# Weight conversion in a fused attention and expert kernel: the shift moved from GpSimd to VectorE, the subtractions from VectorE to GpSimd, and two thirds of the conversions held behind attention blocks

## The chip, the cores and the metric

The kernel runs on one core of a Trainium2 chip. The metric is device time in microseconds (us) of one execution; the number for the kernel before is the median of three runs. The engines are called by the names of the profile: PE is TensorE (PEld its weight loads), DVE is VectorE, ACT is ScalarE, POOL is GpSimd, SP is SyncE.

## What is computed

The reference first runs causal attention with a memory term, then a gated feed-forward layer on its result. Sizes: 4 batches, 8 heads, 576 positions, head size 64; then 2304 rows of 512, hidden width 1536.

```python
scores = scale * q @ k.T;  scores = where(causal, -1e9, scores) - max
local  = softmax(scores) @ v
mem    = (phi(q) @ M_prev) / (phi(q) . z_prev + 1e-6)      # phi(x) = elu(x) + 1
x      = g * mem + (1 - g) * local                        # g = sigmoid(beta), per head
xn     = x / rms(x) * rms_g
out    = (silu(xn @ w_gate) * (xn @ w_val)) @ w_out
```

The three weight matrices arrive as 64-bit floats and are read by the kernel as pairs of 32-bit words.

## The kernel before, in words

**Rows and blocks.** The 2304 rows are 18 blocks of 128. A block goes through: scores on PE (line 449), masking and row minimum on DVE (line 455), exponent on ACT (line 501), a split of the probabilities P into a high and a low f16 part (ACT line 503, then a subtraction in `u_lo`, line 512, on DVE or POOL), a transpose of P, and the product with v (lines 536 to 538). `mem_mm` adds the memory part and `loc_evac` sums the two halves of the heads on POOL (line 611). `x_norm` squares the block on ACT (line 220) and makes the scale on POOL (lines 621 and 624); `x_split` casts the block to two f16 parts, with `hi_cast` on ACT (line 82) and `lo_cast` on DVE (line 85), and transposes it into `xT`. Blocks 0 and 1 are transposed by PE, with an eviction copy (`evict`, lines 348 to 353) that goes to ACT and DVE in turn; all later blocks are transposed by a DMA on SP's queue.

**Feed-forward.** Two blocks form a chunk of 256 rows, so there are 9 chunks. For each of 12 slices of the hidden width `m_proj` makes gate and value (line 765, 24 matmuls), `m_act` and `m_split` the activation in two f16 parts (lines 771 to 775, 796, 797), and `m_down` adds to the output (lines 819 to 821). The first projection needs `xT` of blocks 0 and 1 and the split first third of the gate and value weights.

**Weights.** Gate and value weights come in 24 pieces of 128 x 512, numbered so that pieces 0 to 7, 8 to 15 and 16 to 23 are the three thirds of the hidden width; w_out comes in 12 pieces. A piece is loaded into a ring of 5 slots (`RING`; the load of piece p+5 is issued once piece p has been converted, the first five loads on SP's queue, the rest on ACT's). `f64_to_f32` converts it in three steps: ACT turns the upper words into the float's upper bits (line 690), POOL turns the lower words into 3 bits by a multiplication and a minimum, in place (line 692), DVE shifts and joins both (line 695). Four matmuls on PE (line 135) then sum squares of the piece, which give a scale for the third (`gv_scales`, from line 705). After that `split` (lines 89 to 104) makes two f16 parts. Way "0" is a scaled cast on ACT (line 82) and a subtraction with scale on DVE (line 85). Way "3" is a scaling in place on DVE (line 99), a plain cast on ACT (line 101) and a subtraction on POOL (line 104). `SPLIT` gives the way: in each third of gate and value the pieces alternate between "0" and "3"; all of w_out takes "0". The f16 parts of piece p are written where the f32 data of piece p-1 lay, so the cast of a piece comes after the last read of the piece before it.

**Order.** The attention steps are a list with weights, `A`; the weight and feed-forward steps are emitted in four stretches (`run`, lines 1053 to 1062) and the attention steps between them up to a goal. Attention steps of blocks 0 and 1, then of 2 and 3, get a higher priority (`PRIO`). The tile framework's scheduler fixes the order of each engine's queue from these priorities and its own timing model, so the order of emission is not the order on the engine. `paced` adds an order of its own: a load of piece p after the conversion of piece p-5.

Of the kernel before, what the change touches and what calls it, by code (L numbers as in the profile page):

```python
# [13 lines left out]
U32 = mybir.dt.uint32  # L14
I64 = mybir.dt.int64
AF = mybir.ActivationFunctionType
ALU = mybir.AluOpType
# [14 lines left out]
A3 = 0.2  # L32
A4 = 0.3
C2 = 8
SPLIT = ("03", "03", "03", "0")
VWAY = "11"
RING = 5
PACE = 5
NTP = 2
PRIO = (500, 600, 100)  # L40
NPM = 2
NPOOL = (4, 8)
# [3 lines left out]
def attn_memory_moe_kernel(  # L46
# [12 lines left out]
    nc = tc.nc  # L59
# [7 lines left out]
    NC = DM // P  # L67
# [11 lines left out]


    def hi_cast(dst, src, scale):
        nc.scalar.activation(dst, src, AF.Copy, scale=scale)

    def lo_cast(dst, src, scale, hi):
        nc.vector.scalar_tensor_tensor(
            out=dst, in0=src, scalar=scale, in1=hi, op0=ALU.mult, op1=ALU.subtract
        )

    def split(dst_hi, dst_lo, src, scale, way="0"):


        if way == "0":
            hi_cast(dst_hi, src, scale)
            lo_cast(dst_lo, src, scale, dst_hi)
            return
        if way in "12":
            nc.scalar.activation(src, src, AF.Copy, scale=scale)
        else:
            nc.vector.tensor_scalar(src, src, scale, None, op0=ALU.mult)
        if way in "135":  # L100
            nc.scalar.copy(dst_hi, src)
        else:
            nc.vector.tensor_copy(dst_hi, src)
        nc.gpsimd.tensor_tensor(dst_lo, src, dst_hi, ALU.subtract)
# [69 lines left out]
    blocks = []  # L174
# [150 lines left out]
    def prep_M(b):  # L325
        src = qst.pop(("M", b)).rearrange("p (h e) -> p h e", h=H)
        held.pop(("M", b), None)
        m = sb.tile([P, 2, H, D + 2], F16, tag="M16", name=f"M16_{b}")
        M16[b] = m
        c = consts_of(b) if b < 2 else cb[b]  # L330
        hi_cast(m[:, 0, :, :D], src, c[:, 2:3])
        lo_cast(m[:, 1, :, :D], src, c[:, 2:3], m[:, 0, :, :D])
        nc.gpsimd.tensor_copy(m[:, :, :, D], zhl[:, :, b * H : (b + 1) * H])
# [9 lines left out]
        split(t[:, :, 0, :], t[:, :, 1, :], s3, scale, way)  # L343
        return t

    turn = [0]

    def evict(dst, src):
        turn[0] += 1
        if turn[0] % 2:  # L350
            nc.scalar.copy(dst, src)
        else:
            nc.vector.tensor_copy(dst, src)

    def tposed(dst, src, n):

        if n >= NTP:
            nc.sync.dma_start_transpose(out=dst, in_=src)
            return
        for j0 in range(0, src.shape[1] // P, 4):  # L360
            t = ps.tile([P, 4, P], F32, tag="gv", name="tp")
            for j in range(4):
                w = src[:, (j0 + j) * P : (j0 + j + 1) * P]
                nc.tensor.matmul(t[:, j, :], w, id16, start=True, stop=True)
            evict(dst[:, j0 : j0 + 4, :], t)
# [19 lines left out]
    def prep_q(n):  # L385
        t = split_rows(qst[n], qsc[n][:, 0:1])
        qT[n] = sb.tile([P, 2, H, P], F16, tag="qT", name=f"qT{n}")
        tposed(qT[n][:, 0], flat(t), n)
        if n < NTP:
            for j0 in range(0, H, 4):  # L390
                t = ps.tile([P, 4, P], F32, tag="gv", name="tp")
                nc.tensor.matmul(t, swap16, qT[n][:, 0, j0 : j0 + 4, :], start=True, stop=True)
                evict(qT[n][:, 1, j0 : j0 + 4, :], t)
            return
        nc.sync.dma_start(out=qT[n][D:, 1], in_=qT[n][:D, 0])
        nc.sync.dma_start(out=qT[n][:D, 1], in_=qT[n][D:, 0])
# [107 lines left out]
        Ssb[(n, h0)] = (s, G * w, p16)  # L504

    def lo_on_pool(n, h0):
        return NPOOL[0] <= n < NPOOL[1] and h0 % NPM == 0

    def u_lo(n, h0):
        s, w, p16 = Ssb.pop((n, h0))  # L510
        eng = nc.gpsimd if lo_on_pool(n, h0) else nc.vector
        eng.tensor_tensor(p16[:, w : 2 * w], s[:, :w], p16[:, :w], ALU.subtract)  # L512
        pt = sb.tile([P, 2 * (NI + 1), P], F16, tag="PT", name="PT", bufs=LAG + 1)
        tposed(pt[:, : 2 * w // P, :], p16[:, : 2 * w], n)
        Pt[(n, h0)] = pt
# [111 lines left out]
    def x_split(n):  # L627
        x, ss = t1s.pop(n)
        x16 = sb.tile([P, 2, HD], F16, tag="row16", name="x16")
        hi_cast(x16[:, 0], x, ss)  # L630
        lo_cast(x16[:, 1], x, ss, x16[:, 0])
        c = n // 2
        if n % 2 == 0:
            xT[c] = sb.tile([P, 2 * NC, 2 * P], F16, tag="xT", name=f"xT{c}")
        tposed(xT[c][:, :, (n % 2) * P : (n % 2) * P + P], x16.rearrange("p t d -> p (t d)"), n)
# [6 lines left out]
    raws = {}  # L642
    NR = RING

    begun = {}

    def paced(ins, p):

        if p - PACE in begun:
            tc.add_manual_dep(  # L650
                ins.ins, begun[p - PACE].ins.name,
                mybir.DependencyInfo(mybir.DependencyClass.Sync, mybir.DependencyReason.SCHED_ONLY),
                reason="pace",
            )

    def hold(p, at):

# [4 lines left out]
    def load_w(m, cc, t):  # L662
        w = (w_gate, w_val)[m]
        p = piece(m, cc, t)
        raws[p] = hold(p, 2 * (p % NR))
        ins = (nc.sync if p < PACE else nc.scalar).dma_start(
            out=raws[p].bitcast(I64), in_=w[cc * P : (cc + 1) * P, t * 512 : (t + 1) * 512]
        )
        paced(ins, p)
# [12 lines left out]
    def f64_to_f32(raw, dst, p):  # L682

        r = raw.rearrange("p (f w) -> p f w", w=2)
        ri, di = r.bitcast(I32), dst.bitcast(I32)
        begun[p] = nc.scalar.activation(dst, r[:, :, 1], AF.Prelu, scale=2.0 ** -112, alpha=2.0 ** 32)  # L690

        nc.gpsimd.tensor_scalar(  # L692
            ri[:, :, 0], r.bitcast(U32)[:, :, 0], 2.0 ** -29, 7.0, op0=ALU.mult, op1=ALU.min
        )
        nc.vector.scalar_tensor_tensor(  # L695
            out=di, in0=di, scalar=3, in1=ri[:, :, 0], op0=ALU.logical_shift_left, op1=ALU.bitwise_or
        )

    def way_of(table, third, i):
        return table[third][i % len(table[third])]  # L700
# [39 lines left out]
    def w_split(m, cc, t):  # L740
        p = piece(m, cc, t)
        src = wgv[:, p + 1, :]
        sc = rgs[:, t, m, cc : cc + 1]
        split(wgv16[:, p, :512], wgv16[:, p, 512:], src, sc, way_of(SPLIT, t, p % (2 * NC)))

    def wo_split(f):
        src = wo[:, f + 1, :]
        split(wo16[:, f, :512], wo16[:, f, 512:], src, wos[:, f // 4 : f // 4 + 1], way_of(SPLIT, NT3, f))

# [190 lines left out]
    for s in range(len(units) + LAG + 2):  # L940
        if s < len(units):
            n, h = units[s]
# [25 lines left out]
        if s < len(units):  # L968
            n, h = units[s]
# [172 lines left out]
```

## Time and profile before

| | us |
|---|---|
| three runs | 694.17, 697.15, 700.24 |
| median | 697.15 |
| profiled execution, its time | 696.12 |
| profiled execution, its span | 694.4 |
| busy in the span: PE, DVE, ACT, POOL | 595.0, 478.3, 403.6, 265.4 |
| mean granted PE clock (share of full) | 0.934 |

The span is the time from the first to the last instruction of the profiled execution; 1.7 us of its time lie outside it. Rows of the trace give times in us from the start of the span; durations in groups are in ns as minimum, median and maximum. Idle time before an instruction is shown with what released it.

### The profile page before, as it was taken

How to read it: one execution, taken by the hardware profiler on the slowest of the kernel's cores; microseconds unless marked ns; L12 is line 12 of the kernel's file. 1: busy time of each engine (PE TensorE's matmuls, PEld its weight loads, DVE VectorE, ACT ScalarE, POOL GpSimd, SP SyncE). 2: the span in 40 equal slices, each digit the busy share in tenths (PEclk: the TensorE clock that was granted, in tenths of full speed). 3: DMA queues.
4: the chain of work that ended last, by engine and by line, in shares of the span. 5: the costliest groups of instructions: out<-in, count | busy, mean ns of one | idle time of the engine just before them, and what ended most of it. 6: DMA issues, size and time to landing. Idle time of an engine off the chain costs nothing.

```text
span 694.4 us, 16406 instructions
## 1 busy us (share of the span) xinstructions
PE 595.0 (86%) x6292; PEld 459.8 (66%) x6292; DVE 478.3 (69%) x1427; ACT 403.6 (58%) x831; POOL 265.4 (38%) x312
## 2 busy tenths in 40 slices
PE   2763347586599889999899999999999999999997
PEld 1642235465485568778777778777787778887774
DVE  3898476976588757668787785786887576873221
ACT  5776365765467765767457666766667455442322
POOL 3999987475023333323114231242232221212111
PEclk9975559878699999999999999999999999999999
DMA  8976249732756658863765866366574545341001
GB/s 278 384 247 187 88 131 254 161 84 54 153 122 111 163 107 156 143 131 56 149 136 121 167 136 126 77 104 156 107 147 100 106 84 100 74 78 35 32 1 30
DMA packets 186383, 88.13 MB, mean 127 GB/s; under 512 B 171712, under 2 KB 171712, under 8 KB 186304
## 3 DMA queue, kind: packets, MB, share of 16 engines
q1 hardware_dynamic: 181392, 70.81, 48.3%
q10 hardware_dynamic: 4912, 16.28, 7.4%
q8 instruction: 49, 0.80, 0.5%
q14 instruction: 30, 0.25, 0.1%
HBM read 36.20 MB, written 4.72 MB: 59 GB/s over the span
## 4 chain that ended last, share of the span: by engine, by line
PE 54%; DVE 14%; DMA 13%; ACT 9%; issue 5%; POOL 4%; SPq 1%; ACTq 1%; POOLq 0%; DVEq 0%
PE gv L765 30%; PE out L819 4%; PE out L820 4%; PE out L821 4%; DMA PT<-P 3%; DMA qT<-row 3%; PE sc L449 3%; DVE S L455 2%; PE sc L475 2%; ACT junk L220 2%; POOL wo L692 2%; DVE P L512 2%; DMA kT<-row 2%; DVE wgv L695 1%; DMA zz<-in_z_prev_dram 1%
## 5 line engine op out<-in xcount | busy, mean ns | idle before, releaser
L765 PE MATMUL gv<-xT,wgv 128*128 128x256 f16 x2592 | 363.2, 279 | 16.4 <-DMA xT<-x 9.0
L765 PEld LDWEIGHTS <-wgv 128*128 128x128 f16 x2592 | 253.3, 100 | 59.9 <-DMA xT<-x 9.2
L797 POOL TENSOR_TENSOR h<-th,h 128x256 f16<-128x256 f32 x96 | 70.6, 736 | 272.3 <-ACT h L796 215.5
L501 ACT ACTIVATE S<-S,nm 128x128 f32<-128x128 f32 (+4 forms) x144 | 80.1, 584 | 54.2 <-DVE nm L462 36.4
L449 PE MATMUL sc<-kT,qT 128*128 128x128 f16 x640 | 94.7, 221 | 9.0 <-DVE nm L455 2.9
L512 DVE TENSOR_TENSOR P<-S,P 128x512 f16<-128x512 f32 (+2 forms) x88 | 66.4, 754 | 38.9 <-ACT P L503 38.3
L771 ACT ACTIVATE th<-gv,wt 128x256 f32<-128x256 f32 x108 | 50.2, 467 | 63.9 <-PE gv L765 60.8
L772 DVE SCALAR_TENSOR_TENSOR th<-th,gv 128x256 f32<-128x256 f32 x108 | 44.8, 416 | 60.5 <-ACT th L771 60.1
L455 DVE CUSTOM_DVE_ANT_0 S<-sc,mask,qsc 128x128 f32<-128x128 f32 (+3 forms) x128 | 66.6, 545 | 14.8 <-PE sc L449 13.4
L819 PE MATMUL out<-wo,h 128*128 128x512 f16 x192 | 73.3, 382 | 0.3 <-ACT h L796 0.3
L820 PE MATMUL out<-wo,h 128*128 128x512 f16 x192 | 73.2, 381 | 0.0
L821 PE MATMUL out<-wo,h 128*128 128x512 f16 x192 | 72.2, 381 | 0.8 <-POOL h L797 0.8
L692 POOL TENSOR_SCALAR wo<-wo 128x512 int32<-128x512 uint32 x32 | 68.0, 2126 | 10.1 <-DMA wo<-in_moe_w_out_dram 6.1
L503 ACT CAST P<-S 128x512 f16<-128x512 f32 (+2 forms) x104 | 61.9, 596 | 11.9 <-DMA PT<-P 10.3
L449 PEld LDWEIGHTS <-qT 128*128 128x128 f16 x640 | 55.8, 99 | 16.3 <-DVE nm L455 3.3
L796 ACT CAST h<-th 128x256 f16<-128x256 f32 x96 | 38.3, 400 | 44.9 <-DVE th L775 44.4
L536 PE MATMUL loc<-v,PT 128*128 128x65 f16 x320 | 55.4, 197 | 7.9 <-DMA PT<-P 7.8
L538 PE MATMUL loc<-v,PT 128*128 128x65 f16 x320 | 54.7, 196 | 1.2 <-DVE wt L116 0.9
L537 PE MATMUL loc<-v,PT 128*128 128x64 f16 x320 | 55.0, 197 | 0.0
L775 DVE SCALAR_TENSOR_TENSOR th<-th,wt,gv 128x256 f32<-128x256 f32 x108 | 51.4, 478 | 1.9
L611 POOL TENSOR_TENSOR t<-t,t 128x256 f32<-128x256 f32 x36 | 31.3, 870 | 50.1 <-DVE t L607 38.9
L536 PEld LDWEIGHTS <-PT 128*128 128x128 f16 x320 | 31.5, 100 | 15.0 <-DMA PT<-P 10.4
(228 smaller groups left out, 1087.1 us busy)
## 6 DMA issues: line engine op xcount, KB each, us to landing
kv<-in_qkv_dram SPq DMA_DIRECT2D x18, 512.0 KB, 4.4
wo<-in_moe_w_val_dram ACTq DMA_DIRECT2D x11, 512.0 KB, 4.5
q<-in_qkv_dram SPq DMA_DIRECT2D x18, 256.0 KB, 3.3
wo<-in_moe_w_gate_dram ACTq DMA_DIRECT2D x8, 512.0 KB, 4.7
wo<-in_moe_w_out_dram ACTq DMA_DIRECT2D x8, 512.0 KB, 3.8
qT<-qT SPq DMA_DIRECT2D x32, 128.0 KB, 2.6
out_dram<-res SPq DMA_DIRECT2D x16, 256.0 KB, 2.3
wo<-in_moe_w_gate_dram SPq DMA_DIRECT2D x4, 512.0 KB, 5.3
```

Source lines behind the costliest of these rows:

```text
L449: nc.tensor.matmul(t[:, g * w + j * P : g * w + (j + 1) * P], qT[n][:, t2, h, :], kT[blk_of[(b, j)]][:, h, :], start=(t2 == 0), stop=(t2 = ...
L455: nc.vector.tensor_tensor_reduce(out=s[:, g * w : (g + 1) * w], in0=t[:, g * w : (g + 1) * w], in1=mask[:, m0 : m0 + w], scale=qsc[n][:, 5:6],
L501: nc.scalar.activation(v_, v_, AF.Exp, bias=nm[:, g : g + 1], scale=-1.0)
L503: nc.scalar.copy(p16[:, : G * w], s[:, : G * w])
L512: eng.tensor_tensor(p16[:, w : 2 * w], s[:, :w], p16[:, :w], ALU.subtract)
L536: nc.tensor.matmul(a, phi_, vhi, start=(j == 0), stop=False)
L692: nc.gpsimd.tensor_scalar(ri[:, :, 0], r.bitcast(U32)[:, :, 0], 2.0 ** -29, 7.0, op0=ALU.mult, op1=ALU.min)
L765: nc.tensor.matmul(o, lhs, xT[c][:, rhs, :], start=(cnt == 0), stop=(cnt == 3 * NC - 1))
L797: nc.gpsimd.tensor_tensor(h16[:, 1], th, h16[:, 0], ALU.subtract)
L819: nc.tensor.matmul(o, hh, whi, start=(f == 0), stop=False)
L820: nc.tensor.matmul(o, hh, wlo, start=False, stop=False)
L821: nc.tensor.matmul(o, hl, whi, start=False, stop=(f == NF - 1))
```

## The change

Five edits:

- The conversion's lower words are shifted right by 29 on DVE instead of being multiplied on POOL (36 pieces).
- `SPLIT` is "3" everywhere: 12 of the 24 gate and value pieces and all 12 of w_out go from way "0" to way "3".
- `evict` always uses ACT.
- The P subtractions of blocks 2 and 3 (8 of 128 x 512) go from DVE to POOL.
- The first step of the conversion (ACT) of pieces 8 to 15 is ordered behind the ACT cast of block 0's x in `x_split`, and of pieces 16 to 23 behind that of block 1's. Both are ACT instructions.

```diff
-SPLIT = ("03", "03", "03", "0")
+SPLIT = ("3", "3", "3", "3")
...
     def hi_cast(dst, src, scale):
-        nc.scalar.activation(dst, src, AF.Copy, scale=scale)
+        return nc.scalar.activation(dst, src, AF.Copy, scale=scale)
...
-    turn = [0]
-
     def evict(dst, src):
-        turn[0] += 1
-        if turn[0] % 2:
-            nc.scalar.copy(dst, src)
-        else:
-            nc.vector.tensor_copy(dst, src)
+        nc.scalar.copy(dst, src)
...
     def lo_on_pool(n, h0):
-        return NPOOL[0] <= n < NPOOL[1] and h0 % NPM == 0
+        return n in (2, 3) or NPOOL[0] <= n < NPOOL[1] and h0 % NPM == 0
...
-        hi_cast(x16[:, 0], x, ss)
+        xdone[n] = hi_cast(x16[:, 0], x, ss)
...
-    begun = {}
+    begun, xdone = {}, {}
...
         if p - PACE in begun:
-            tc.add_manual_dep(
-                ins.ins, begun[p - PACE].ins.name,
-                mybir.DependencyInfo(mybir.DependencyClass.Sync, mybir.DependencyReason.SCHED_ONLY),
-                reason="pace",
-            )
+            after(ins, begun[p - PACE], "pace")
+
+    def after(ins, before, why):
+        tc.add_manual_dep(
+            ins.ins, before.ins.name,
+            mybir.DependencyInfo(mybir.DependencyClass.Sync, mybir.DependencyReason.SCHED_ONLY),
+            reason=why,
+        )
...
         begun[p] = nc.scalar.activation(dst, r[:, :, 1], AF.Prelu, scale=2.0 ** -112, alpha=2.0 ** 32)
-
-        nc.gpsimd.tensor_scalar(
-            ri[:, :, 0], r.bitcast(U32)[:, :, 0], 2.0 ** -29, 7.0, op0=ALU.mult, op1=ALU.min
-        )
+        if 2 * NC <= p < 6 * NC:
+
+            after(begun[p], xdone[p // (2 * NC) - 1], "first blocks")
+        nc.vector.tensor_scalar(ri[:, :, 0], ri[:, :, 0], 29, None, op0=ALU.logical_shift_right)
```

## Rows read from the trace of the kernel before

**Rows 1.** Busy time by stage: window, then each engine's busy us (instructions), clock, DMA

```profile
0.00:98.00 98.00, 45.09 (x413) 31.96 (x414) 68.76 (x230) 60.94 (x123) 81.05 (x76) 0.72 0.65 218
98.00:260.00 162.00, 127.33 (x1213) 94.14 (x1213) 117.97 (x336) 100.75 (x207) 73.40 (x77) 0.89 0.64 138
260.00:684.00 424.00, 417.09 (x4638) 330.72 (x4636) 290.69 (x862) 239.79 (x498) 109.80 (x159) 1.00 0.52 104
```

**Rows 2.** The same view in stretches of 20 us: PE, PEld, DVE, ACT, POOL

```profile
20.00:40.00 20.00, 14.31 (x162) 11.36 (x163) 17.83 (x48) 16.68 (x34) 19.33 (x20) 0.90 0.90 337
40.00:60.00 20.00, 12.71 (x138) 9.40 (x137) 19.83 (x73) 13.13 (x28) 19.27 (x10) 0.67 0.67 210
60.00:80.00 20.00, 5.95 (x38) 3.32 (x37) 9.83 (x25) 10.18 (x16) 19.18 (x16) 0.50 0.60 184
80.00:100.00 20.00, 8.15 (x59) 5.38 (x58) 15.09 (x44) 11.57 (x22) 16.58 (x15) 0.50 0.24 72
```

**Rows 3.** The chain that ended last, 55 to 130 us: start, us, what

```profile
71.06 1.98 POOL wo L692
...
78.50 0.53 POOL xs L624
...
98.06 3.78 PE gv L765 x21
```

**Rows 4.** Timeline of DVE: second half of block 0's heads leaves PSUM

```profile
51.93 0.40 DVE L607 TENSOR_TENSOR t<-loc,fl 128x256 f32<-128x256 f32 x1
```

**Rows 5.** Timeline of POOL, 56 to 99 us

```profile
56.43 2.01 POOL L611 TENSOR_TENSOR t<-t,t 128x256 f32<-128x256 f32 x1
58.53 6.70 POOL L692 TENSOR_SCALAR wo<-wo 128x512 int32<-128x512 uint32 x3
...
78.46 0.57 POOL L624 TENSOR_TENSOR xs<-xs,mhalf 128x1 f32<-128x1 f32 x1
...
97.28 1.15 POOL L104 TENSOR_TENSOR wgv<-wgv 128x512 f16<-128x512 f32 x1
```

**Rows 6.** Timeline of ACT: the casts of block 0's and block 1's x

```profile
79.06 0.72 ACT L82 ACTIVATE x<-t,xs 128x512 f16<-128x512 f32 x1 [1.79 <-POOL xs L624]
...
94.43 0.70 ACT L82 ACTIVATE x<-t,xs 128x512 f16<-128x512 f32 x1
```

**Rows 7.** Lines of the conversion, to 260 us: ns min/median/max, first to last start us

```profile
L692 POOL TENSOR_SCALAR wo<-wo x32: 1962/2010/2514, 14.0 to 127.3; 128x512 int32<-128x512 uint32 x32
L695 DVE SCALAR_TENSOR_TENSOR wgv<-wgv,wo x24: 655/685/1126, 16.7 to 90.1; 128x512 int32<-128x512 int32 x24
L690 ACT ACTIVATE wgv<-wo x24: 640/664/689, 14.6 to 76.6; 128x512 f32<-128x512 f32 x24
```

**Rows 8.** Lines of the two ways of splitting, same columns

```profile
L104 POOL TENSOR_TENSOR wgv<-wgv x12: 1146/1158/1658, 65.5 to 157.4; 128x512 f16<-128x512 f32 x12
L85 DVE SCALAR_TENSOR_TENSOR wgv<-wgv,rgs x12: 715/744/1119, 59.8 to 155.6; 128x512 f16<-128x512 f32 x12
L85 DVE SCALAR_TENSOR_TENSOR wo<-wo,wos x12: 742/750/1425, 204.1 to 227.8; 128x512 f16<-128x512 f32 x12
L99 DVE TENSOR_SCALAR wgv<-wgv,rgs x12: 459/473/893, 56.6 to 136.4; 128x512 f32<-128x512 f32 x12
L82 ACT ACTIVATE wgv<-wgv,rgs x12: 704/721/724, 55.2 to 153.4; 128x512 f16<-128x512 f32 x12
L101 ACT CAST wgv<-wgv x12: 602/618/628, 60.6 to 156.7; 128x512 f16<-128x512 f32 x12
```

**Rows 9.** Evictions of the PE transposes, first and last of five groups on DVE, one on ACT

```profile
L353 DVE CAST qT<-tp x4: 676/678/692, 25.7 to 36.8; 128x512 f16<-128x512 f32 x4
L353 DVE CAST xT<-tp x2: 670/680/691, 81.3 to 97.3; 128x512 f16<-128x512 f32 x2
L351 ACT CAST qT<-tp x4: 564/576/586, 26.1 to 36.5; 128x512 f16<-128x512 f32 x4
```

**Rows 10.** P subtractions of blocks 2 and 3 on DVE, 100 to 180 us

```profile
L512 DVE TENSOR_TENSOR P<-S,P x8: 676/692/1643, 125.7 to 161.1; 128x512 f16<-128x512 f32 x8
```

## The prediction, made before the changed kernel ran

> **What bounds the kernel now.** I read the busy times by stage first. From 260 to 684 us PE is busy 417 of 424 us at the full clock of 2.4 GHz [rows 1]: that stage has no room, and nothing in the change takes work from PE. In the first 98 us PE is busy only 45 us and POOL 81; between, from 98 to 260, PE is busy 127 of 162. So the change can win only by letting the last stage begin earlier. The stretches of 20 us say which engine holds the start: POOL is busy 19.3, 19.3 and 19.2 of 20 us from 20 to 80, DVE is nearly full only from 20 to 60 (17.8 and 19.8) and falls to 9.8, and PE waits at a granted clock of 0.50, its lower level of 1.2 GHz, from 60 to 100 [rows 2]. The chain of waits runs from 69.7 to 90 us over POOL's instructions, the conversion's L692 among them, and reaches the first projection at 98.06 [rows 3].
>
> The timelines show how one queue does this. The second half of block 0 leaves PSUM on DVE at 51.93 [rows 4], but its sum starts on POOL at 56.43, behind conversions; then three conversions (6.70 us) and more stand ahead of the two small steps for its scale, the last of which starts at 78.46 [rows 5]. ACT casts block 0's x at 79.06 and block 1's at 94.43 [rows 6]. The same queue delays the splitting of the first third of the weights: its first cast is at 55.2 and its last POOL subtraction at 97.28 [rows 5, 8]. So both things that the first projection needs come out of POOL's queue at about 97 us.
>
> **The change part by part.**
>
> *Shift to DVE.* POOL loses 36 instructions of 2.01 us = 72.4 us [rows 7]. The trace has no plain shift on DVE. Nearest from below is the scaling of a contiguous 128x512 tile, 0.459 us at its shortest [rows 8]; from above the join at its longest, 1.126. An added instruction can't cost less than nothing here, since nothing else in the edit shortens the join. I take the join's median, 0.685, because it reads the same strided integer words: 36 x 0.685 = +24.7 us on DVE (16.5 to 40.5).
>
> *More splits in way "3".* 24 splits lose a DVE subtraction (12 x 0.744 + 12 x 0.750 = 17.9 us), gain a DVE scaling (24 x 0.473 = 11.4; by its longest, 0.893, 21.4) and a POOL subtraction (24 x 1.158 = 27.8), and ACT saves 24 x (0.721 - 0.618) = 2.5 [rows 8].
>
> *P subtractions of blocks 2 and 3.* DVE loses 8 x 0.692 = 5.5 us [rows 10], POOL gains 8 x 1.158 = 9.3 (the row of the same shape). At most 8 x 0.466 = 3.7 us longer on the path of these blocks, at best nothing, since DVE's queue gets shorter. I take nothing.
>
> *Evictions.* DVE loses 14 x 0.678 = 9.5 us, ACT gains 14 x 0.576 = 8.1 [rows 9]. ACT has 10 of 40 us free from 20 to 60 [rows 2], and conversions held back free 0.664 each [rows 7]. I take nothing; without that cover it costs up to 8 us before the start.
>
> Sums: POOL -72.4 + 27.8 + 9.3 = -35.3 us; DVE +24.7 - 17.9 + 11.4 - 5.5 - 9.5 = +3.2 (-5 to +29); ACT +8.1 - 2.5 = +5.6. POOL's queue, the one that holds the start, loses its big instructions, and DVE pays little overall.
>
> *The holds.* ACT already has an order, so a hold places 16 conversions behind two casts in ACT's own queue. Behind a held conversion stand the ACT-issued loads five pieces on, and on DVE and PE the shift, join and sums of squares of the same piece. SP's queue is not touched. Ahead of x(0), DVE no longer does the joins of pieces 8 and up. The price is that the ring stands full until x(0). 24 conversions ran from 14.6 to 76.6, 2.7 us apiece [rows 7]. After x(0) five pieces lie ready and 11 loads remain, 11 x 2.7 = 30 us, then shift and join, 1.4 us. The last join was at 90.1 [rows 7]. So the hold costs nothing if x(0) comes by 90.1 - 31.4 = about 59 us.
>
> *When the start comes.* x(0): from 51.93 + 0.40 on DVE [rows 4], a sum of 2.01 at most [rows 5], a square and two small POOL steps of about 1.5 together (estimate): about 56, instead of 79.06. That is before 59. x(1) came 15.4 us after x(0) [rows 6] with POOL's backlog in between: at most 71, and the projection 3.6 later (94.43 to 98.06), at most 75. Splits of the first third: the f16 parts overwrite the piece before, so cast and subtraction alternate, 8 x (0.618 + 1.158) = 14.2 us from 55.2: 69.4. DVE's work in the first 98 us was 68.8; less 16 joins (11.0) and the evictions (9.5), plus 8 shifts (5.5), it is 53.8, which fits into 70 us if the held conversions stay behind. I take a first projection at 70: -28 us (62 to 85, that is -36 to -13).
>
> *After the start.* The second third can be split from about 75 on and the third from about 95, long before the 157.4 at which the last subtraction now starts [rows 8], so chunk 0 doesn't wait for weights any more. w_out's splits, now from 204.1 to 227.8, 2.15 us each, go from 0.722 + 0.750 to 0.618 + 1.158 in the same alternation, and up to 0.618 + 1.658: +0.3 to +0.8 each, 4 to 10 us over 12 if nothing covers them [rows 8]. PE has other work between them; I take +3, bounds 0 and +10.
>
> By the Trainium skill ("SBUF — State Buffer", section on the two separate sides) DVE instructions with two SBUF inputs and POOL instructions share a port pair, and whoever starts first keeps it for its whole instruction; 32 more POOL subtractions could then stop DVE for up to 32 x 1.158 = 37 us. The trace does not show blocks of that size: with POOL busy 19.3 of 20 us [rows 2], against instructions of 2.01 us, the join's median is 0.685 and its longest 1.126 [rows 7], 0.44 above. 32 x 0.44 = 14 us bounds that price by the rows, most of it beside other work.
>
> *Sum.* The profiled execution took 696.1 (span 694.4 and 1.7 outside). 696.1 - 28 + 3 = 671. The median of the runs shown is 1 above that execution: 672.
>
> **The rivals.** *DVE becomes the bound of the start.* It was 95% busy from 20 to 60 [rows 2]. With shifts and scalings near their upper bounds, first-third shifts cost 8 x 1.126 = 9.0 instead of 5.5, and the second third's conversions (8 x (1.126 + 0.685) = 14 us) get between the steps of block 1. Then the start comes at about 70 + 3.5 + 8.5 = 82, and the time is 684. Against it: attention of blocks 0 and 1 has the higher priority.
>
> *The gain is absorbed before 260.* There PE is idle for 35 us [rows 1], so this stage is partly held by the attention of blocks 2 and 3, their transposes by DMA and their loads. If those keep their places, PE only waits longer: of 28 us some 5 remain, less 3 for w_out's splits, 695. Against it: DVE is busy 118 of 162 us there and gets 5.5 + 6.5 us lighter by P and the splits, and these steps stand behind blocks 0 and 1 in the same queues.
>
> *The holds bind (slower).* If block 0's x stays where it is, at 79, because ACT's or DVE's order and not POOL's queue sets it, conversions resume at 79 and the last join comes at 79 + 31.4 = 110, 20 us later than now; scales and splits of the last third follow, and the time is 717. It decides from x(0) at 59 on, and each us later costs one. For it: the order on the engines is fixed ahead from a timing model, which may misjudge the wait. Against it: x(0) waited 27 us behind its last DVE input, and what stood between were POOL's conversions.
>
> **How the numbers follow.** Forecast 0.60 (own range 655 to 685), DVE-bound 0.17, absorbed 0.12, holds bind 0.11. A measurement of this kernel tells about 1%, 7 us, from no change. Faster by more: 0.60 + 0.17 + 0.02 of the absorbed case = 0.79; within: 0.10; slower: 0.11. The range reaches down to 650 (a start at 62 and 14 us of the idle PE time won) and up to 697, so that it leaves out the holds and little else.
>
> **What would show it.** Right: x(0)'s cast at 52 to 60 and x(1)'s at 62 to 72 in ACT's timeline; the first projection at 65 to 75; POOL below 12 of 20 us from 20 to 60; the shift's group on DVE at 0.46 to 1.1 us; the last join before 95; the granted clock below 1.00 for a shorter time. Wrong: x(0) at 70 or later with DVE full and POOL idle (DVE-bound), the first projection at 70 but block 2's and 3's x where they were (absorbed), joins after 100 with PE waiting for splits (holds). w_out's splits lasting over 30 us would show that term mis-sized.

## The result, and the profile after

The changed kernel takes 687.7 us, the median of four runs (687.09 to 689.58), against 696.7 for the kernel before on the same chip (four runs, 694.17 to 700.24): a ratio of 0.9872 [0.9824, 0.992], 1.3% faster. I had forecast 672, a gain of 25 us; 9 came. The profiled execution took 687.62 us (span 685.9).

The two groups of the conversion on DVE over the whole profile after (ns minimum, median, maximum; first to last start in us; form):

```profile
L691 DVE TENSOR_SCALAR wo<-wo x32: 405/421/1381, 13.4 to 123.8; 128x512 int32<-128x512 int32 x32
...
L692 DVE SCALAR_TENSOR_TENSOR wgv<-wgv,wo x24: 670/685/1419, 15.2 to 96.7; 128x512 int32<-128x512 int32 x24
```

The shift's median is 0.421 us, less than my lower bound. But some took up to 1.381: the mean is 0.60, and all 36 took 21.1 us together. The join kept its median of 0.685 [rows 7], and its last start moved from 90.1 to 96.7.

ACT's timeline after answers to [rows 6]:

```profile
55.99 0.72 ACT L82 ACTIVATE x<-t,xs 128x512 f16<-128x512 f32 x1 [1.02 <-POOL xs L618]
56.62 0.61 ACT L101 CAST wgv<-wgv 128x512 f16<-128x512 f32 x1
57.12 2.56 ACT L97 ACTIVATE kv<-kv,cb 128x512 f32<-128x512 f32 x4
59.59 2.88 ACT L687 ACTIVATE wgv<-wo 128x512 f32<-128x512 f32 x5
...
77.89 0.71 ACT L82 ACTIVATE x<-t,xs 128x512 f16<-128x512 f32 x1
...
163.08 0.72 ACT L82 ACTIVATE x<-t,xs 128x512 f16<-128x512 f32 x1
```

Block 0's cast is at 55.99 instead of 79.06. Then come the five conversions that the hold had kept in the ring (L687 at 59.59, five instructions in a row). Block 1's cast follows 21.9 us after block 0's, where before it was 15.4.

POOL's timeline after, rows that answer to [rows 5]:

```profile
53.13 0.73 POOL L605 TENSOR_TENSOR t<-t,t 128x256 f32<-128x256 f32 x1 [5.40 <-DVE t L601]
...
62.72 3.51 POOL L605 TENSOR_TENSOR t<-t,t 128x256 f32<-128x256 f32 x1 [0.36 <-DVE t L601]
...
68.54 1.60 POOL L104 TENSOR_TENSOR wgv<-wgv 128x512 f16<-128x512 f32 x1
...
89.61 1.49 POOL L104 TENSOR_TENSOR wgv<-wgv 128x512 f16<-128x512 f32 x1 [3.37 <-ACT wgv L101]
```

POOL now waits for block 0's sum (5.40 us idle before it) instead of having it wait. The last row is the eighth and last subtraction of the first third, which came at 97.28 when only four of them were on POOL.

DVE's timeline after, between the two halves of block 1's heads leaving PSUM (both L601), and the two later scales of the weights (L714):

```profile
62.23 0.42 DVE L601 TENSOR_TENSOR t<-loc,fl 128x256 f32<-128x256 f32 x1
62.56 3.09 DVE L692 SCALAR_TENSOR_TENSOR wgv<-wgv,wo 128x512 int32<-128x512 int32 x5
66.98 0.61 DVE L691 TENSOR_SCALAR wo<-wo 128x512 int32<-128x512 int32 x1 [1.34 <-DMA wo<-in_moe_w_val_dram]
67.70 1.42 DVE L692 SCALAR_TENSOR_TENSOR wgv<-wgv,wo 128x512 int32<-128x512 int32 x1
69.05 1.37 DVE L691 TENSOR_SCALAR wo<-wo 128x512 int32<-128x512 int32 x1
...
73.63 0.42 DVE L601 TENSOR_TENSOR t<-loc,fl 128x256 f32<-128x256 f32 x1
...
83.56 0.35 DVE L714 TENSOR_SCALAR rgs<-rg,wt 128x4 f32<-128x4 f32 x2
...
132.63 0.77 DVE L714 TENSOR_SCALAR rgs<-rg,wt 128x4 f32<-128x4 f32 x2
```

This is where the start was lost. Between 62.6 and 73.6 DVE does the second third's joins and shifts, and before 66.98 it stands idle 1.34 us for a load that was issued only when a conversion had freed its slot. The second half of block 1's heads waits behind all that in the same queue. ACT has a part in it: its evictions of block 1's transposed P (`PT`, L347) start at 65.49 and 67.49, behind released conversions.

PE's timeline after, from block 1's cast to the first projection:

```profile
78.66 0.61 PE L358 MATMUL tp<-wo,x 128*128 128x128 f16 x4 [2.22 <-ACT x L82]
81.50 0.61 PE L358 MATMUL tp<-wo,x 128*128 128x128 f16 x4 [2.24 <-DVE x L85]
83.09 0.61 PE L135 MATMUL csum<-wgv 128*128 128x128 bf16 x4 [0.98 <-DVE wgv L692]
...
84.68 0.60 PE L135 MATMUL csum<-wgv 128*128 128x128 bf16 x4 [0.34 <-DVE wgv L692]
85.08 7.01 PE L762 MATMUL gv<-xT,wgv 128*128 128x256 f16 x47
```

The transposes of block 1's low part wait 2.24 us for DVE (0.65 before), and the projection stands behind sums of squares (L135) of pieces of the last third, released by block 1's own cast, which wait for their joins. So it comes 7.2 us after block 1's cast; before it was 3.6.

The stages of the profile after, cut at the first projection and at the casts of x of blocks 3, 4 and 6 (window; busy us of PE, PEld, DVE, ACT, POOL with instructions; clock, DMA share, GB/s), as in [rows 1]:

```profile
0.00:85.30 85.30, 41.22 (x395) 30.93 (x396) 63.18 (x232) 63.11 (x131) 28.29 (x53) 0.78 0.63 219
85.30:163.00 77.70, 54.28 (x503) 41.81 (x502) 64.64 (x164) 45.04 (x91) 45.61 (x42) 0.76 0.73 177
163.00:223.90 60.90, 54.06 (x497) 38.31 (x497) 42.98 (x128) 37.16 (x82) 35.60 (x39) 0.92 0.60 109
223.90:280.00 56.10, 53.75 (x581) 40.15 (x580) 38.55 (x116) 38.97 (x81) 22.75 (x30) 1.00 0.81 162
```

And in 20 us stretches, as in [rows 2]:

```profile
20.00:40.00 20.00, 12.22 (x144) 10.16 (x144) 13.86 (x44) 16.83 (x33) 5.28 (x11) 1.00 0.91 342
40.00:60.00 20.00, 11.13 (x128) 8.67 (x128) 16.97 (x75) 16.97 (x37) 5.13 (x9) 0.68 0.25 77
60.00:80.00 20.00, 8.49 (x64) 5.83 (x64) 17.58 (x44) 14.43 (x30) 14.38 (x13) 0.50 0.60 211
80.00:100.00 20.00, 12.15 (x88) 8.66 (x89) 20.00 (x47) 13.15 (x24) 7.77 (x6) 0.67 0.67 219
...
120.00:140.00 20.00, 16.35 (x201) 14.26 (x199) 19.85 (x60) 13.09 (x28) 12.41 (x10) 0.91 0.81 171
```

POOL fell from 19.3 to about 5 of 20 us in the stretches from 20 to 60. DVE, which had been free from 60 on (9.8 of 20), is now the full engine: 17.6, then 20.0.

The same four cuts in the profile before are at 98.06, 171.63, 227.08 and 288.90. Up to the cast of block 6 PE did 1972 matmuls in both; from there to the end of the span it took 405.5 us before and 405.9 after. So the whole difference lies ahead of that cast, and it sums up:

| stretch | before | after | change | forecast |
|---|---|---|---|---|
| to the first projection | 98.06 | 85.08 | -13.0 | -28 |
| to x of block 3 | 73.57 | 78.00 | +4.4 | 0 |
| to x of block 6 | 117.27 | 116.94 | -0.3 | +3 |
| to the end of the span | 405.5 | 405.9 | +0.4 | 0 |
| sum | | | -8.5 | -25 |

### The profile page after: what moved, and what is told of

Read it like the earlier page. It is cut to its first block, busy times and chain, and to the rows that moved or that the text cites. A ratio compares the mean times of both kernels' runs of the same rounds, so it can differ in the third digit from the quotient of the medians.

```text
span 685.9 us, 16422 instructions
## 1 busy us (share of the span) xinstructions
PE 597.1 (87%) x6292; PEld 461.3 (67%) x6292; DVE 480.8 (70%) x1441; ACT 406.9 (59%) x845; POOL 232.3 (34%) x308
## 4 chain that ended last, share of the span: by engine, by line
PE 43%; DVE 17%; DMA 16%; ACT 13%; issue 5%; POOL 4%; SPq 1%; ACTq 0%; DVEq 0%; POOLq 0%
PE gv L762 23%; DMA kv<-in_qkv_dram 6%; DMA PT<-P 5%; PE out L816 4%; PE out L817 4%; PE out L818 4%; DVE S L449 3%; ACT junk L220 2%; PE sc L443 2%; DMA qT<-row 2%; ACT P L497 2%; PE sc L469 2%; ACT S L495 2%; DVE P L506 2%; DMA phT<-row 2%
## 5 line engine op out<-in xcount | busy, mean ns | idle before, releaser
L506 DVE TENSOR_TENSOR P<-S,P 128x512 f16<-128x512 f32 (+2 forms) x80 | 61.0, 763 | 40.4 <-ACT P L497 39.7
L443 PEld LDWEIGHTS <-qT 128*128 128x128 f16 x640 | 56.6, 100 | 21.9 <-issue 8.0
L605 POOL TENSOR_TENSOR t<-t,t 128x256 f32<-128x256 f32 x36 | 31.4, 873 | 60.0 <-DVE t L601 57.7
L530 PEld LDWEIGHTS <-PT 128*128 128x128 f16 x320 | 31.6, 100 | 14.2 <-DMA PT<-P 10.8
L104 POOL TENSOR_TENSOR wgv<-wgv 128x512 f16<-128x512 f32 x24 | 31.7, 1321 | 26.8 <-ACT wgv L101 26.6
```

The lines of the kernel that those rows point to most:

```text
L443: nc.tensor.matmul(t[:, g * w + j * P : g * w + (j + 1) * P], qT[n][:, t2, h, :], kT[blk_of[(b, j)]][:, h, :], start=(t2 == 0), stop=(t2 = ...
L530: nc.tensor.matmul(a, phi_, vhi, start=(j == 0), stop=False)
```

## The experiments

For every run the table has the ratio to the kernel before and, from ACT's and PE's timelines of its profile, the casts of x of blocks 0, 1, 3 and 6 and the first run of the projection. The projection's start is that of the first run of more than one matmul. From the cast of block 6 to the end all sixteen profiles took 404.8 to 407.7 us, so that column decides the time of the profiled execution. Comparisons between runs are made by their ratios, since one execution need not be typical: those of e3, e4 and e12 took some 5 us more than the median of their runs, that of e7 some 4 less.

How far the same program varies can be read too. In the traces of e7 and e10 all computing instructions stand on their engines in the same order as in the changed kernel and in e6; these are repeats. e6 in turn has the changed kernel's order up to 190 us. So four profiles of one order give the projection at 84.36 to 85.29 and block 3's x at 160.02 to 163.09, and the ratios of the two pairs differ by 0.2 and 0.6% (4 us). A smaller difference between two runs of different series is not told from none.

| run | ratio [interval] | x 0 | x 1 | projection | x 3 | x 6 |
|---|---|---|---|---|---|---|
| before | 1 | 79.06 | 94.43 | 98.06 | 171.63 | 288.90 |
| after | 0.9872 [0.9824, 0.992] | 55.99 | 77.89 | 85.08 | 163.08 | 280.02 |
| e1 shift only | 0.9961 [0.9931, 0.9991] | 66.76 | 92.50 | 98.06 | 181.54 | 289.47 |
| e2 holds only | 0.9914 [0.9859, 0.997] | 56.58 | 89.59 | 97.54 | 173.34 | 285.28 |
| e9 shift and holds | 0.9928 [0.9891, 0.9965] | 58.51 | 80.93 | 86.94 | 164.66 | 281.84 |
| e3 no holds | 0.9861 [0.981, 0.9912] | 61.10 | 85.65 | 91.34 | 173.33 | 286.19 |
| e4 both held to x 1 | 1.0067 [1.0028, 1.0105] | 56.24 | 72.11 | 78.86 | 183.80 | 299.28 |
| e5 shift on POOL | 1.0209 [1.0167, 1.0251] | 57.37 | 93.22 | 102.17 | 187.31 | 303.60 |
| e6 w_out way "0" | 0.9789 [0.9757, 0.9822] | 55.84 | 77.74 | 84.93 | 162.32 | 274.68 |
| e7 C2 = 0 (order as after) | 0.9854 [0.9815, 0.9893] | 56.21 | 78.10 | 85.29 | 160.02 | 276.77 |
| e8 P on DVE | 0.9879 [0.9836, 0.9922] | 55.71 | 77.61 | 84.79 | 165.84 | 281.82 |
| e12 evictions in turn | 0.9934 [0.9895, 0.9973] | 58.32 | 81.49 | 88.62 | 173.27 | 289.82 |
| e10 w_out way "0", C2 = 0 (order as e6) | 0.9729 [0.9678, 0.978] | 55.28 | 77.17 | 84.36 | 163.09 | 273.18 |
| e11 w_out way "0", third third held | 0.9861 [0.9807, 0.9914] | 61.10 | 79.52 | 85.02 | 172.04 | 282.96 |
| e13 w_out without join | 0.9773 [0.9715, 0.9832] | 54.75 | 76.66 | 83.84 | 160.65 | 273.04 |
| e14 w_out short loads | 0.9807 [0.9754, 0.9861] | 55.02 | 76.92 | 84.11 | 160.25 | 277.68 |

### Which edit brought the gain

**e1**, the kernel before with the shift on DVE:

```diff
-        nc.gpsimd.tensor_scalar(
-            ri[:, :, 0], r.bitcast(U32)[:, :, 0], 2.0 ** -29, 7.0, op0=ALU.mult, op1=ALU.min
-        )
+        nc.vector.tensor_scalar(ri[:, :, 0], ri[:, :, 0], 29, None, op0=ALU.logical_shift_right)
```

> The kernel before with the shift on VectorE and nothing else of the change. Theory A (POOL's big instructions held the start, so the shift is the heart of the change): block 0's x is cast at 55 to 65 us instead of 79.1, the first projection comes at 80 to 90, the time is 684 to 691. Rival B (the holds do it, by keeping 16 conversions out of the way of blocks 0 and 1; the shift alone only moves the crowd from POOL to VectorE): VectorE is full from 20 to 60, x(0) at 65 to 75, the first projection after 90, the time is 692 to 699.

Measured 0.9961. Block 0's x came 12.3 us earlier, block 1's only 1.9, the first projection not at all. Taking POOL's big instructions away is not enough: the wait moves to DVE. The second half of block 0's heads left PSUM at 61.71 there (51.93 before), and the later conversions, w_out's among them, and their waits for loads (2.07 us before 74.77) stand in DVE's timeline ahead of block 1's heads.

**e2**, the kernel before with the holds, the shift still on POOL:

```diff
+        if 2 * NC <= p < 6 * NC:
+            after(begun[p], xdone[p // (2 * NC) - 1], "first blocks")
```

> The kernel before with the two holds and nothing else of the change; the shift stays on POOL. Theory A: POOL has only 8 of its 2.0 us instructions before x(0), so x(0) comes at 56 to 62, but 16 of them, 32 us, then stand between x(0) and the last third, so the last join is at 105 to 115 and the time is 694 to 704. Rival B: nearly all of the gain is there, 684 to 690.

Measured 0.9914. Block 0's x came at 56.58, as early as in the whole change; block 1's was 33 us behind it, with eight released conversions of 2.0 us and more on POOL in between (64.65 to 87.25 in its timeline).

**e9**, both in the kernel before and nothing else (the diffs of e1 and e2 together).

> The kernel before with the shift on VectorE and the holds, and none of the other edits. Alone the shift gave a ratio of 0.996 and the holds 0.991. Theory A (two ways to keep the same POOL instructions out of block 0's way, so they overlap; the added subtractions bring little): x(0) at 54 to 58, x(1) at 74 to 82, and the time within 3 us of the changed kernel, 685 to 691. Rival (the subtractions on POOL are what makes room on VectorE for the shift): 692 to 697.

Measured 0.9928: no more than the holds alone, though the first projection came 10.6 us earlier than there. For block 0 the two edits overlap: its x comes at 56.58 with the holds alone and at 58.51 with both. Of the 10.6 us, 8.7 were left at block 3's x and 3.4 at block 6's; what took the rest was not followed.

The other edits bring more than these two. e10, whose order is e6's, adds to e9 the splits of the gate and value weights, the evictions and P; in the same series it took 679.04 us, e9 691.48. P shows no worth (e8). How the 12 us divide between the splits and the evictions is not shown, as no run has these splits alone.

**e3**, the changed kernel without the holds:

```diff
-        if 2 * NC <= p < 6 * NC:
-            after(begun[p], xdone[p // (2 * NC) - 1], "first blocks")
```

> The changed kernel without the two holds. Theory D (in the changed kernel the conversions released by the holds stand between x(0) and x(1) on VectorE; without holds they stand before x(0) instead): x(0) at 60 to 70, x(1) at 74 to 82, so the first projection hardly moves, 82 to 90, and the time is 684 to 692. Theory M (the holds push the weight loads into the stretch from 100 to 140 us where the transposes by DMA of blocks 2 and 3 run): without holds the phT transpose that took 10.9 us takes under 7, block 2's x is cast before 146, and the time is 677 to 683.

Measured 0.9861, the same as with them. In the profiled execution the first projection came 6.3 us later and block 6's x 6.2, but that execution was the slowest of four (693.35 us; the others 685.62 to 688.45). Beside the other edits these runs show no worth of the holds.

**e5**, the changed kernel with the shift back on POOL (the diff of e1 the other way).

> The changed kernel with the shift back on POOL; splits in way 3, the P subtractions, the evictions and the holds stay. Theory A (with the added subtractions the shift can't stay on POOL): between x(0) and the first projection POOL has 16 conversions of 2.0 us and 16 or so subtractions of 1.2 to 1.6 us, over 50 us of work, so the first projection comes at 98 or later and the time is 694 to 704. Rival B (holds are what counts, and they alone gave 0.991): the time stays at 687 to 692.

Measured 1.0209, slower than the kernel before. With 32 more subtractions on POOL the shift can't stay there: block 1's x came at 93.22 and the first projection at 102.17.

### What held the start

**e4**, the changed kernel with pieces 8 to 15 also held to block 1's x:

```diff
-            after(begun[p], xdone[p // (2 * NC) - 1], "first blocks")
+            after(begun[p], xdone[1], "first blocks")
```

> The changed kernel, with pieces 8 to 15 also held behind the cast of block 1's x. Theory D: with nothing between them x(1) follows x(0) by 10 to 14 us instead of 21.9, so it is cast at 66 to 70 and the first projection is at 74 to 78; the second third comes later, its last join at 86 to 90 and the last third's at 100 to 106; the time is 680 to 690. Theory M: loads move still later, the transposes of block 2 and 3 take longer and the time is 690 to 700 although the start is earlier.

Measured 1.0067. The same three timelines in this run, first ACT's casts of x of blocks 0 and 1:

```profile
56.24 0.72 ACT L82 ACTIVATE x<-t,xs 128x512 f16<-128x512 f32 x1 [1.04 <-POOL xs L618]
...
72.11 0.70 ACT L82 ACTIVATE x<-t,xs 128x512 f16<-128x512 f32 x1
```

DVE's, with the two halves of block 1's heads and the second third's scale:

```profile
62.48 0.41 DVE L601 TENSOR_TENSOR t<-loc,fl 128x256 f32<-128x256 f32 x1
...
65.94 0.42 DVE L601 TENSOR_TENSOR t<-loc,fl 128x256 f32<-128x256 f32 x1
...
111.13 0.36 DVE L714 TENSOR_SCALAR rgs<-rg,wt 128x4 f32<-128x4 f32 x2
```

And POOL's, with the sum of block 1's first half:

```profile
64.57 0.72 POOL L605 TENSOR_TENSOR t<-t,t 128x256 f32<-128x256 f32 x1
```

Without released conversions the two halves leave PSUM 3.5 us apart instead of 11.4, and the sum takes 0.72 us instead of 3.51 (which the path did not wait for, as the second half left later still). ACT evicts `PT` at 62.95 and 63.72 instead of 65.49 and 67.49. Block 1's x follows block 0's by 15.9 us instead of 21.9: the released second third cost 6 us there, by way of DVE's queue and ACT's. That part of the explanation is shown.

The run also shows that an early projection is not yet an early end. It began 6.2 us sooner than in the changed kernel, and the time was 2% longer. The second third's scale moved from 83.56 to 111.13, and PE's waits from 80 to 185 us (us in total, times, longest) say what followed:

```profile
PE csum L135 <- DVE wo L692: 6.3, 3, 3.3
PE loc L530 <- DMA PT<-P: 6.2, 3, 3.1
PE gv L762 <- ACT wgv L101: 6.0, 3, 4.4
PE csum L135 <- DVE wgv L692: 5.6, 5, 2.7
```

17.9 us of waits for joins and splits stand in PE's queue, and block 3's x, behind them, came 111.7 us after block 1's; in the changed kernel it was 85.2.

**e12**, the changed kernel with the evictions in turn again:

```diff
-        nc.scalar.copy(dst, src)
+        turn[0] += 1
+        if turn[0] % 2:
+            nc.scalar.copy(dst, src)
+        else:
+            nc.vector.tensor_copy(dst, src)
```

> The changed kernel with the evictions going to ACT and VectorE in turn as before. I priced that edit at nothing, with up to 8 us of ACT time before the start if its cover is gone. Theory (ACT delays the first third's casts, which took 30 us from the first cast to the last subtraction where I had 14.2): the first projection comes 2 to 5 us earlier, 80 to 83, the time is 683 to 687. Rival (VectorE is the dearer engine from 20 to 60): x(0) later than 58, the time 689 to 694.

Measured 0.9934, some 4 us slower than the changed kernel by the ratios, with intervals that overlap. Block 0's x came 2.3 us later and the first projection 3.5, more than the repeats differ (0.9), so this edit, priced at nothing, probably won something at the start. What it won in time is not settled.

**e8**, the changed kernel with the P subtractions of blocks 2 and 3 back on DVE:

```diff
-        return n in (2, 3) or NPOOL[0] <= n < NPOOL[1] and h0 % NPM == 0
+        return NPOOL[0] <= n < NPOOL[1] and h0 % NPM == 0
```

> The changed kernel with the P subtractions of blocks 2 and 3 back on VectorE (8 of 128 x 512). I priced this edit at nothing. Theory D (VectorE bounds the stretch of blocks 2 and 3): moving 5.5 us back onto it costs 2 to 5 us, 690 to 693. Rival (the longer POOL subtraction, 1.2 to 1.9 us in the changed kernel, stands on the path of P and its transpose): 683 to 686. Neither: within 2 us of 687.7.

Measured 0.9879, not told from the changed kernel: worth nothing that shows, as priced.

### Behind the start

**e6**, the changed kernel with w_out's splits in way "0" again:

```diff
-SPLIT = ("3", "3", "3", "3")
+SPLIT = ("3", "3", "3", "0")
```

> The changed kernel with w_out's 12 splits in way 0 as before. My term for them in the prediction was +3 us (0 to 10). Theory A (the term is real): the time is 682 to 685. Rival (PE has other work there; in the changed kernel's profile PE waits for a w_out split only once, 0.4 us): no difference beyond 2 us, 686 to 690.

Measured 0.9789, 0.8% less than the changed kernel, and the same up to block 3's x. In the same series e7, the changed kernel's order again, took 687.52 us and e6 683.16. First and last of the twelve subtractions in POOL's timeline of the changed kernel:

```profile
193.45 1.33 POOL L104 TENSOR_TENSOR wo<-wo 128x512 f16<-128x512 f32 x1
...
222.86 1.15 POOL L104 TENSOR_TENSOR wo<-wo 128x512 f16<-128x512 f32 x1
```

And of the twelve on DVE in e6's:

```profile
194.38 0.74 DVE L85 SCALAR_TENSOR_TENSOR wo<-wo,wos 128x512 f16<-128x512 f32 x1
...
216.02 0.75 DVE L85 SCALAR_TENSOR_TENSOR wo<-wo,wos 128x512 f16<-128x512 f32 x1 [0.27 <-ACT wo L82]
```

On POOL the splits come every 2.67 us, on DVE every 1.97. From block 3's x to block 6's the changed kernel takes 117.0 us, e6 112.4. Yet PE's direct wait for these splits is only 0.4 us in the changed kernel; the rest comes by way of what stands in the same queues, and which of it is not settled.

**e7**, the changed kernel with all of w_out's conversion steps emitted in the later stretch, and **e10**, the same with e6's edit:

```diff
-C2 = 8
+C2 = 0
```

> The changed kernel with all of w_out's conversions emitted after the stretch of the projections of slices 8 to 11 (the constant C2 is 0 instead of 8), which takes 8 of 12 shifts and joins, some 8 us of VectorE, and their loads out of the attention of blocks 2 and 3. Theory D (VectorE's queue holds blocks 2 and 3 between 85 and 163 us): x(3) is cast at 150 to 158 instead of 163 and the time is 679 to 684. Rival W (that stretch is held by PE's own queue, which waits for the splits of the second and third third and for transposes): x(3) within 3 us of 163, the time 685 to 690; w_out coming too late would show as more than 692.

> The changed kernel with w_out's splits in way 0 (that alone gave 683.2) and w_out's conversions emitted later (C2 is 0; that alone moved x(3) from 163.1 to 160.0 but not the median, 687.5). If both gains are real and separate: x(3) at 159 to 161, x(4) at 212 to 216 and 679 to 682. If the later conversions only push the wait into the stage of w_out's splits: 683 to 687.

e7 measured 0.9854 and e10 0.9729, 679.04 us, the fastest of all and faster than both kernels. But the edit moves only the order of emission, and the scheduler put every computing instruction back where it had stood. ACT's first conversion step of w_out (ns, first to last start) in e6:

```profile
L687 ACT ACTIVATE wo<-wo x8: 656/674/694, 96.1 to 126.1; 128x512 f32<-128x512 f32 x8
L687 ACT ACTIVATE wo<-rawo x4: 657/666/690, 120.3 to 147.2; 128x512 f32<-128x512 f32 x4
```

and in e10:

```profile
L687 ACT ACTIVATE wo<-wo x8: 656/666/682, 95.5 to 126.3; 128x512 f32<-128x512 f32 x8
L687 ACT ACTIVATE wo<-rawo x4: 659/666/677, 122.2 to 148.0; 128x512 f32<-128x512 f32 x4
```

So these two runs tested neither of their theories: e7 repeats the changed kernel, and e10 confirms e6. The 3 us at block 3's x in e7 and the 4 us between e10 and e6 are what one order varies by. These are the two middle stages of e10 (to x of block 3, to x of block 4), to lay beside the second and third of the changed kernel:

```profile
84.60:163.10 78.50, 53.05 (x503) 40.37 (x502) 64.82 (x164) 45.13 (x92) 44.34 (x42) 0.78 0.71 174
163.10:215.30 52.20, 48.17 (x450) 34.72 (x450) 41.68 (x125) 37.32 (x77) 19.82 (x27) 0.91 0.63 128
```

The first is unchanged. The second is 8.7 us shorter (6.7 in e6), with POOL at 19.8 us instead of 35.6, without w_out's splits.

**e11**, e6 with pieces 8 to 15 free and 16 to 23 held to block 1's x:

```diff
-        if 2 * NC <= p < 6 * NC:
-            after(begun[p], xdone[p // (2 * NC) - 1], "first blocks")
+        if 4 * NC <= p < 6 * NC:
+            after(begun[p], xdone[1], "first blocks")
```

> The changed kernel with w_out's splits in way 0, pieces 8 to 15 free and only pieces 16 to 23 held, behind block 1's x. Theory D (conversions between x(0) and x(1) on VectorE and ACT cost 6 us of the start, conversions before x(0) cost 5 us of x(0)): x(0) at 58 to 62, x(1) at 72 to 78, the first projection at 80 to 85; the last third comes later than now. If the start counts, 678 to 682; if the stretch after it is held by the readiness of the weights, as the kernel with all held to x(1) suggests, 684 to 692.

Measured 0.9861, against 0.9789 for e6. The third third's last subtraction came at 152.06 instead of 159.17 in e6, but block 0's x fell back to 61.10 and block 3's to 172.04: earlier splits of the third third did not by themselves bring block 3 forward.

**e13 and e14** ask what holds the stretch from the projection to block 3's x, where DVE is full for two of the 20 us stretches shown and the DMA engines are busy 73%.

```diff
+        if p < 6 * NC:
             nc.vector.tensor_scalar(ri[:, :, 0], ri[:, :, 0], 29, None, op0=ALU.logical_shift_right)
             nc.vector.scalar_tensor_tensor(
...
+        k = DM // 4 if at in (7, 11) else DM
-        ins = nc.scalar.dma_start(out=r.bitcast(I64), in_=w_out[f * P : (f + 1) * P, :])
+        ins = nc.scalar.dma_start(out=r.bitcast(I64)[:, :k], in_=w_out[f * P : (f + 1) * P, :k])
```

e13 (the first edit) leaves out the shift and join of w_out's 12 pieces, so w_out keeps only its upper words. e14 (the second) loads only a quarter of five of w_out's pieces, 0, 2, 3, 5 and 9, where the expectation counts six: 2.0 MB less and not 2.4. Both also change the order on the engines from 94 us on.

> The changed kernel without shift and join for w_out's 12 pieces: w_out keeps only its upper words, so the output is not the reference's. That takes 24 instructions, 12 x (0.42 + 0.69) = 13 us, off VectorE between 92 and 151 us, and leaves every load as it is. Theory D (VectorE holds the stretch from the first projection to block 3's x): x(3) is cast at 152 to 158 instead of 163 and the time is 678 to 684. Rival M (the transposes by DMA hold it): x(3) within 3 us of 163, the time within 3 us of 687.7.

> The changed kernel with six of w_out's twelve loads cut to a quarter of their columns, among them those of pieces 0, 2, 3 and 5 (the rest of those pieces is stale data, so the output is not the reference's): 2.4 MB of 13.9 less between 85 and 163 us, with every instruction of the engines as it is. Theory M (loads delay the transposes of blocks 2 and 3, phT by 10.9 us, and PE, ACT wait for them): the phT transpose of block 2 takes under 8 us, x(3) is cast at 154 to 160 and the time is 679 to 685. Theory D: x(3) within 3 us of 163, 685 to 690.

e13 measured 0.9773 and e14 0.9807, some 7 and 4 us less than the changed kernel, the second hardly more than the repeats differ. From the projection to block 3's x they took 76.8 and 76.1 us, where the four profiles of one order took 74.7 to 78.7. So neither DVE's work on w_out nor these loads alone set block 3's x, and what does stays open. (e13's gain lies behind it: 112.4 us to block 6's x instead of 116.9; it was not followed.) Whether the loads delay a transpose is not shown. From 98 to 112 us the changed kernel's DMA issues have (us from issue to landing)

```profile
phT<-row SPq DMA_TRANSPOSE x1, 10.9
```

and e14's

```profile
phT<-row SPq DMA_TRANSPOSE x1, 5.0
```

But in e7, with the changed kernel's order and all its loads, the same transpose landed after 5.1.

## Why the prediction was right, and where it failed

**Right.** POOL's queue held block 0's x: with the conversions held back it came at 55.99, forecast about 56, and at 56.58 with nothing but the holds (e2). It did not alone hold the first projection: with all conversions off POOL (e1) that stayed at 98.06. The sums of busy time came near what I worked out: POOL -33.1 us (forecast -35.3), DVE +2.5 (+3.2), ACT +3.3 (+5.6). For DVE that is luck: the shifts took 21.1 us (24.7) and the added scalings 17.6 (11.4), and these misses largely cancel. From block 6's cast on nothing changed. P cost nothing that shows (e8). The time fell inside the range, on the faster side. Of the signs, x(0) and POOL (5.3 and 5.1 of 20 us) came; x(1), the projection, the shift's median and the last join (96.7) lay outside theirs.

**The step that failed** is "When the start comes": 70 was forecast, 85.1 came, and that 15.1 is nearly the whole miss. It falls into three:

- I added up to "at most 75" and then took 70: 5 us that no row carried.
- "x(1) came 15.4 us after x(0) [rows 6] with POOL's backlog in between: at most 71." It came 21.9 after, 6.5 more. e4 shows 6 of it to be the second third's conversions, which the hold releases at the very cast of block 0 and so into the queues of block 1. The price was named in the rival (8.5 us) and left out of the forecast. e4 shows also that the 15.4 does not shrink by taking the conversions away: 15.9 remained. Before, the sum of block 1's second half stood 3.8 us behind conversions on POOL (86.45 to 90.23); in e4 it stood 2.1 us behind the first third's subtractions there (66.36 to 68.47).
- "[...] and the projection 3.6 later [...]". It was 7.2: PE waited 2.24 us for DVE's low part of x, which had DVE's queue before it, where it had waited 0.65, and 0.98 and 0.34 for joins of pieces that block 1's cast had released. The sums of squares of the same pieces, which I had listed as standing behind the held conversions, I did not follow to PE's queue.

The splits of the first third, 14.2 us by my sum, took 34.5 (first cast 56.62, last subtraction 89.61 and 1.49), with waits in ACT's and POOL's queues; but the projection began before they were done, so they did not set its start.

My check that DVE's work fits into 70 us rested on "if the held conversions stay behind". Behind block 0 they do, ahead of block 1 they don't. The rival "DVE becomes the bound of the start" (82, 684 us) was the nearest. Its mechanism from block 0's x on is what the trace shows; its other half, an expensive shift of the first third, is not: a median of 0.421 against the 0.685 I took and 1.126 as bound.

**"After the start"** failed more mildly. The third third was to be split from 95 on, since its joins would be done. Its scale was written at 132.63, 35 us after its last join, about where it was before (134.15); so it was not the data that it waited for. It waited in PE's queue: DVE had reduced the sums of squares by 99.65 (L707), but the two small matmuls that come next (L122) ran at 120.18, behind scores and projections, some of which waited for DMA transposes. The stretch up to block 3's x grew by 4.4 us, a part of the rival "absorbed". DVE was at 20.0 and 19.85 of 20 us in two parts of it and the granted clock at 0.67 from 80 to 100, so it had less room than the sums over 162 us showed; but taking w_out's shifts and joins off DVE did not shorten it (e13). What in it sets block 3's x was not settled (e11, e13, e14).

**w_out's splits** I priced at +3 (0 to 10). e6 says 4.6 us by the profiles, 4.4 against e7 and some 6 by the ratios: in the bounds, undersized. The -0.3 in the table hides this: without these splits (e6) the stretch from block 3's x to block 6's is 4.9 us shorter than before, and what won that was not followed. The sign that I gave for it, over 30 us, showed: 193.45 to 224.01.

**The evictions**, priced at nothing, were probably a gain at the start, and perhaps one of some 4 us in time (e12).

**The holds.** The sum by which the hold costs nothing if x(0) comes by about 59 had the last join at 31.4 us after x(0), that is at 87.4; it was at 96.7. I had counted all sixteen pieces from block 0's x, but the last eight wait for block 1's, at 77.89. The rival in which they bind did not come, since its condition, x(0) at 79, did not. e4 shows how near it lay: held a little longer, the kernel is slower than before.

**The rule of the Trainium skill** that I weighed ("SBUF — State Buffer", section "SBUF: two separate sides": DVE instructions with two SBUF inputs and POOL instructions lock a shared port pair, and the loser blocks for the whole instruction) I had looked at from DVE's side only, and put at nothing in the sum. On POOL's side the trace agrees: its sum of 0.72 us took 3.51 beside five joins without a gap and ended 0.6 us after the last. On DVE's side it now agrees too: the join at 67.70 took 1.42 us beside POOL's subtractions.

The shifts, with one input, were held as well, like the one at 69.05. The 19 of them that ran beside no POOL instruction took at most 0.433 us, the other 17 up to 1.381. For the shifts, joins and scalings together the time above the undisturbed median is some 16 us, where it was 3 before; that is near the 14 that I had taken as bound. How much of it lay on the path was not measured; 2.6 us of it stand between the two halves of block 1's heads (67.70, 69.05 and a scaling at 71.13).

## What to carry to other kernels

When an engine's queue is cleared, follow the freed and the held work to the next queue: work held behind a milestone is released at that milestone, into the queues of whatever comes next. Work out each milestone by its own row up to the end, and don't take less than the sum says. A shift or subtraction moved off one engine is priced per stage: way "3" lost some 4 to 6 us for w_out, where POOL's subtraction stood in a tight alternation with ACT's cast, so try such an edit stage by stage, as e6 did. And check in the trace that an edit changed the order on the engines before reading anything from its time (e7, e10).

## What the runs showed of the hardware

A shift of 128x512 integers at a stride of two words took 0.421 us on DVE (the median), where POOL's multiplication and minimum took 2.010 [rows 7]. Beside POOL instructions the same shift took up to 1.381 us, without them at most 0.433. A POOL addition of two 128x256 tiles took 3.51 us while DVE ran five joins in a row, and 0.72 without them. The same DMA transpose, in the same order of instructions and with the same loads, landed after 10.9 us in one execution and 5.1 in another.
